# Two groups instead of three: regrouping products and blocks in a Strassen-type FFN step

## The chip, the cores and the metric

The kernel runs on one core of one Trainium2 chip. The metric is the device time of one execution in microseconds (us), of which the lower is the better. TensorE (PE in the profile; PEld is its weight loads) does the matmuls, VectorE (DVE) and ScalarE (ACT) read their results from PSUM, GpSimd (POOL) works on SBUF only, and SyncE (SP) issues the DMAs. Each engine takes its instructions in order and waits on semaphores of the others.

## The reference

A chunked attention (chunks of 64 tokens) gives 2304 tokens of 512 features. Two feed-forward layers follow; the change lies in the second, "FFN 2", a mixture of 8 experts over all tokens:

```python
logits = x @ w_gate
P = np.exp(logits - logits.max())
for _ in range(8):                      # Sinkhorn scaling: rows, then columns
    P /= P.sum(1, keepdims=True) + 1e-09
    P /= P.sum(0, keepdims=True) + 1e-09
    P *= N / E
out = np.zeros((N, D))
for e in range(E):                      # E = 8, hidden width 1024
    h = np.maximum(x @ w1[e], 0.0)
    out += P[:, e:e + 1] * (h @ w2[e])
```

All is in float32. A matmul of full precision is made of three matmuls of rounded parts: high with high, high with low, low with high.

## The kernel before

The 2304 tokens are cut into 6 blocks of 384, and FFN 2 takes them in 3 pairs of blocks. Each pair runs 32 steps (`k` counts on through the pairs), one for a quarter of an expert's hidden units: 256 of them. The first layer of a step, 256 hidden units by 2 blocks of tokens, is computed by seven matrix products of a Strassen-Winograd scheme instead of eight (`product(ps, k, i)`, i from 0 to 6, 6 matmuls each with 384 columns). The second layer of the first pair is plain: six blocks of 128 tokens by 512 features (`layer2_ffn2`, 6 matmuls of 512 columns each). The later pairs use another scheme (`step2`), which the change doesn't touch.

The function `step(k, y, hooks)` writes one step of the first pair. The order of the source is the order on each engine: the schedule is written by hand, with no planner behind it. A step computes the products of its own first layer and the six blocks of the second layer of the step before, `y(0)` to `y(5)`; so relu and splitting have most of a step's time.

- Products 0, 3 add up in PSUM tile `pa`, products 1, 4, 6 in `pb`, products 2, 5 in `pd`. In between, other engines read the tile: ACT copies `pa` after product 0 into `p1` (L739) and `pd` after product 2 into `p7` (L750), DVE adds `pb` and `p1` into `p16` after product 1 (L743) and into `p165` after product 4 (L759). The next product on the tile has to wait for that reader. The three tiles are the same three PSUM banks in each step.
- The four results of the first layer are `pa` itself after product 3, `c21` (L762), `c22` (L764) and `c12` (L774). `relu_split` makes a high part of each by ACT (L685, `gh`) and a low part by DVE (L686, `gl`).
- A block `y(n)` takes one of three PSUM buffers; DVE adds it to the output sums `acc` with the expert's weight of each token (L721, or L712 and L714 for the first two experts; in step 8 also a scaling by ACT, L705).
- `hook(0)` to `hook(9)` run small tasks handed in by the main loop. In most steps these are, for the weights of the next step: hook 0 a cast (with POOL's subtraction and a store by SP) of half of the second layer's weights and a copy of the first layer's raw weights to PSUM (L512); hook 1 one cast; hook 2 the other half and four sums by DVE (L524 to L527); hook 3 a copy to PSUM (L572) and a cast; hook 4 two casts; hook 5 four sums by DVE (L579 to L582) and a cast; hook 6 three casts; hook 7 two; hook 8 one. A cast is an ACT instruction for the high part and a POOL subtraction for the low part, both under L204 and L205, and the result goes to DRAM by an SP store, as the later pairs load it from there.
- Other hooks bring tasks of a few steps only: the Sinkhorn scaling of the gate in steps 2 to 8 (`sinkhorn_rows`, L1095 to L1099, five DVE operations, in hook 5 of steps 3, 5 and 7; `sinkhorn_cols` with a small matmul L1103), and the splitting of the second pair's x in steps 24 to 31 (`x_tasks2`, in hooks 6 and 8: sums by DVE, L650 and L652 among them, and a cast under L204).

Of the kernel before, what the change touches and what calls it, by code (L numbers as in the profile page):

```python
# [39 lines left out]
def block_attention_two_ffn_kernel(ctx, tc, shape, qk, v, w_in, w_out, w_gate, w1, w2, out, out_t):  # L40
# [74 lines left out]
    def f(ap):  # L115
        return ap.bitcast(F32)
# [368 lines left out]
    def ffn1_out(i):  # L485
        layer2_ffn1(*at(i))
        sum_ffn1(*at(i))
# [186 lines left out]
    def product(ps, k, i):  # L674
        w, (bh, bl) = wc[k, PRODUCTS[i][0]], xc[k // NU2, PRODUCTS[i][1]]
        for kk in range(2):
            for s, (a, b) in enumerate(((0, bh), (0, bl), (1, bh))):
                nc.tensor.matmul(  # L678
                    ps, w[:, a, kk, :], b[:, kk, :],
                    start=(i < 3 and kk == 0 and s == 0), stop=(kk == 1 and s == 2), skip_group_check=(i >= 3),  # L680
                )

    def relu_split(key, src):
        g2[key] = hi, lo = tuple(gp.tile([P, TB], F32R, tag=t, name=t) for t in ("gh", "gl"))
        nc.scalar.activation(hi, src, AF.Relu)  # L685
        nc.vector.scalar_tensor_tensor(lo, src, 0.0, f(hi), ALU.max, ALU.subtract)  # L686
# [3 lines left out]
    def layer2_ffn2(k, j, t, new_y=pyp.tile):  # L690

        p, u = divmod(k, NU2)
        e, b = u // UPE, 2 * p + j
        T = b * TT + t
        o = slice(t * 512, (t + 1) * 512)
        py = new_y()
        mm3(
            py,
            [(tuple(a[:, t * P:(t + 1) * P] for a in g2[k, i, j]), w2t[NU1 + k, i]) for i in range(2)],
            6,  # L700
        )
        if u == 0 and t == 0:
            acc[b] = new_acc(b)
        if p == 0 and u == 2 * UPE - 1:
            nc.scalar.activation(acc[b][:, o], acc[b][:, o], AF.Copy, scale=pm[:, T, 0:1])  # L705
        if p == 0 and u == UPE and t == 0:
            acc1[b] = new_x(1).rearrange("p k t -> p (k t)").bitcast(F32)
        a = acc[b][:, o]
        if p == 0 and e < 2:
            a = (acc, acc1)[e][b][:, o]  # L710
            if u % UPE == 0:
                nc.vector.tensor_copy(a, py)  # L712
            else:
                nc.vector.tensor_tensor(a, py, a, ALU.add)  # L714
            return
        if p == 0 and u == 2 * UPE + j * TT + t:
            nc.vector.scalar_tensor_tensor(a, acc1[b][:, o], pm[:, T, 1:2], a, ALU.mult, ALU.add)
        if u == 0:
            nc.vector.tensor_scalar(a, py, pm[:, T, 0:1], None, ALU.mult)
        else:  # L720
            nc.vector.scalar_tensor_tensor(a, py, pm[:, T, e:e + 1], a, ALU.mult, ALU.add)  # L721
        if u == NU2 - 1:
            nc.sync.dma_start(out=out[T * P:(T + 1) * P, :], in_=a)

    def step(k, y, hooks):

        t32 = lambda tag, bufs=3: tmp.tile([P, TB], F32, tag=tag, name=tag, bufs=bufs)  # L730
        tt = nc.vector.tensor_tensor
        hook = lambda n: [h() for h in hooks.get(n, ())]
        pa = new_h()
        product(pa, k, 0)
        hook(0)
        if k == 0:
            y(0)
        p1 = t32("s1")
        nc.scalar.copy(p1, pa)  # L739
        pb = new_h()  # L740
        product(pb, k, 1)
        p16 = t32("t", 2)
        tt(p16, pb, p1, ALU.add)  # L743
        hook(1)
        if k == 0:
            y(1)
        pd = new_h()
        product(pd, k, 2)
        p7 = t32("s1")
        nc.scalar.copy(p7, pd)  # L750
        hook(2)
        if k:
            y(0)
        hook(3)
        product(pa, k, 3)
        relu_split((k, 0, 0), pa)
        product(pb, k, 4)
        p165 = t32("t", 2)
        tt(p165, pb, p1, ALU.add)  # L759
        product(pd, k, 5)  # L760
        c21 = pd
        tt(c21, pd, p16, ALU.add)  # L762
        c22 = t32("z")
        tt(c22, p165, p7, ALU.add)  # L764
        relu_split((k, 1, 0), c21)
        relu_split((k, 1, 1), c22)
        hook(4)
        if k:
            y(1)
        y(2)  # L770
        hook(5)
        product(pb, k, 6)
        c12 = pb
        tt(c12, pb, p1, ALU.add)  # L774
        relu_split((k, 0, 1), c12)
        hook(6)
        y(3)
        hook(7)
        y(4)
        hook(8)  # L780
        y(5)
        hook(9)
# [465 lines left out]
    for k in range(NU2):  # L1248
        hooks = {}
        hook = lambda n, task: hooks.setdefault(n, []).append(task)  # L1250
        if k == 0:
# [3 lines left out]
            y = lambda n: ffn1_out(NS1 - LAG + n)  # L1255
        else:
            y = lambda n: layer2_ffn2(k - 1, n // TT, n % TT)
# [30 lines left out]
        for n in range(10):  # L1288
            if (k, n) in steps:
                hook(n, steps[k, n])  # L1290
        step(k, y, hooks)
    yx.close()
    y2x = ExitStack()
# [63 lines left out]
```

## Time and profile before

| what | value |
|---|---|
| runs | 1914.67, 1915.0, 1915.12 us; median 1915.0 us |
| profiled execution | 1914.93 us, span 1913.1 us |
| granted TensorE clock, mean | 0.998 |
| PE busy | 1889.2 us (99%) |
| DVE busy | 1542.4 us (81%) |
| POOL busy | 1369.0 us (72%) |
| ACT busy | 890.0 us (47%) |

The 32 steps of the first pair run from 450 us to 963 us of the span. A time of a matmul in the trace is its latency; matmuls overlap, so the cost of a group is read from the start of its first matmul to the start of the next group's first. In a time line, like instructions that follow each other stand in one row with their number, and a note in brackets tells how long the engine had been idle and who released it.

### The profile page before, as it was taken

How to read it: one execution, taken by the hardware profiler on the slowest of the kernel's cores; microseconds unless marked ns; L12 is line 12 of the kernel's file. 1: busy time of each engine (PE TensorE's matmuls, PEld its weight loads, DVE VectorE, ACT ScalarE, POOL GpSimd, SP SyncE). 2: the span in 40 equal slices, each digit the busy share in tenths (PEclk: the TensorE clock that was granted, in tenths of full speed). 3: DMA queues.
4: the chain of work that ended last, by engine and by line, in shares of the span. 5: the costliest groups of instructions: out<-in, count | busy, mean ns of one | idle time of the engine just before them, and what ended most of it. 6: DMA issues, size and time to landing. Idle time of an engine off the chain costs nothing.

```text
span 1913.1 us, 35096 instructions
## 1 busy us (share of the span) xinstructions
PE 1889.2 (99%) x11522; PEld 1821.7 (95%) x11522; DVE 1542.4 (81%) x2575; ACT 890.0 (47%) x2043; POOL 1369.0 (72%) x1400
## 2 busy tenths in 40 slices
PE   6999999999999999999999999999999999999998
PEld 5999999999899889999999999999999999999998
DVE  8998787866898887778858888888777888777777
ACT  6877777765555555555532222232223222222322
POOL 5635767665666766667767778787778877777776
PEclk9999999999999999999999999999999999999999
DMA  7411111103788888888898888888888888888883
GB/s 265 136 65 45 45 45 45 40 17 117 286 293 301 307 306 301 304 297 305 295 354 286 257 252 260 262 262 258 253 258 259 261 281 274 253 261 262 262 252 121
DMA packets 256997, 430.49 MB, mean 225 GB/s; under 512 B 26000, under 2 KB 81328, under 8 KB 256816
## 3 DMA queue, kind: packets, MB, share of 16 engines
q1 hardware_dynamic: 256816, 428.25, 68.2%
q8 instruction: 93, 1.52, 0.3%
q14 instruction: 88, 0.72, 0.1%
HBM read 304.89 MB, written 123.26 MB: 224 GB/s over the span
## 4 chain that ended last, share of the span: by engine, by line
PE 92%; DVE 5%; POOL 1%; ACT 1%; issue 1%; DMA 1%; DVEq 0%; SPq 0%; POOLq 0%; ACTq 0%
PE h L678 36%; PE y L837 23%; PE y L370 23%; PE h L370 9%; DMA raw<-in_moe_w_in 1%; DVE sm L303 0%; PE t L370 0%; DVE ex L294 0%; DVE mx L286 0%; DVE x L355 0%; DVE s L418 0%; DVE cvm L188 0%; POOL gl L205 0%; DVE s L442 0%; DVE s L413 0%
## 5 line engine op out<-in xcount | busy, mean ns | idle before, releaser
L678 PE MATMUL h<-x,wa 128*128 128x384 f32 x4032 | 789.8, 335 | 0.0
L678 PEld LDWEIGHTS h<-x,wa 128*128 128x128 f32 x4032 | 709.0, 188 | 9.7 <-issue 0.6
L837 PE MATMUL y<-gh,wb 128*128 128x384 f32 x1764 | 519.1, 334 | 1.4 <-DVE acc L842 0.6
L842 DVE TENSOR_TENSOR acc<-y,acc 128x768 f32<-128x768 f32 x367 | 348.9, 953 | 133.8 <-PE y L837 132.5
L205 POOL TENSOR_TENSOR gl<-cvm,gh 128x384 fp32r<-128x384 f32 x252 | 261.7, 1038 | 137.8 <-ACT gh L204 137.8
L837 PEld LDWEIGHTS y<-gh,wb 128*128 128x128 f32 x1764 | 324.8, 188 | 3.8 <-ACT gh L204 1.9
L837 PE MATMUL y<-gl,wb 128*128 128x384 f32 x882 | 294.7, 334 | 0.0
L204 ACT CAST gh<-cvm 128x384 fp32r<-128x384 f32 x252 | 129.3, 513 | 293.4 <-DVE cvm L873 166.0
L204 ACT CAST gh<-z 128x384 fp32r<-128x384 f32 x189 | 97.0, 513 | 347.0 <-POOL z L889 225.6
L370 PE MATMUL y<-wb,gh 128*128 128x512 f32 x768 | 238.9, 392 | 0.0
L205 POOL TENSOR_TENSOR gl<-z,gh 128x384 fp32r<-128x384 f32 x189 | 197.8, 1047 | 45.4 <-ACT gh L204 40.4
L370 PE MATMUL h<-x,wa 128*128 128x384 f32 x1152 | 216.3, 336 | 0.4 <-DVE t L428 0.3
L370 PEld LDWEIGHTS h<-x,wa 128*128 128x128 f32 x1152 | 200.2, 188 | 1.6 <-DVE t L428 0.8
L370 PE MATMUL y<-gh,wb 128*128 128x384 f32 x708 | 194.4, 336 | 0.8 <-DVE acc L481 0.8
L423 POOL TENSOR_TENSOR s<-s,s 128x384 f32<-128x384 f32 x91 | 95.4, 1049 | 103.4 <-DVE s L418 76.4
L370 PEld LDWEIGHTS y<-wb,gh 128*128 128x128 f32 x768 | 142.4, 188 | 25.6 <-issue 0.4
L837 PEld LDWEIGHTS y<-gl,wb 128*128 128x128 f32 x882 | 165.6, 188 | 0.0
L370 PE MATMUL y<-wb,gl 128*128 128x512 f32 x384 | 151.2, 394 | 0.0
L205 POOL TENSOR_TENSOR wa<-cvm,wa 128x256 fp32r<-128x256 f32 x128 | 99.6, 778 | 67.3 <-ACT wa L204 64.4
L370 PEld LDWEIGHTS y<-gh,wb 128*128 128x128 f32 x708 | 129.1, 188 | 3.0 <-issue 1.9
L685 ACT ACTIVATE gh<-h 128x384 fp32r<-128x384 f32 x96 | 47.2, 492 | 178.2 <-DVE h L774 97.5
L370 PE MATMUL y<-gl,wb 128*128 128x384 f32 x354 | 118.3, 334 | 0.0
(224 smaller groups left out, 3119.0 us busy)
## 6 DMA issues: line engine op xcount, KB each, us to landing
wa<-w1d SPq DMA_DIRECT2D x448, 256.0 KB, 3.1
wb<-w2d SPq DMA_DIRECT2D x441, 256.0 KB, 3.1
w1d<-wa SPq DMA_DIRECT2D x224, 256.0 KB, 3.2
w2d<-wb SPq DMA_DIRECT2D x192, 256.0 KB, 3.6
raw<-in_moe_w SPq DMA_DIRECT2D x33, 512.0 KB, 4.1
wb<-in_moe_w SPq DMA_DIRECT2D x62, 256.0 KB, 4.8
qk<-in_qk SPq DMA_DIRECT2D x18, 512.0 KB, 4.9
raw<-in_moe_w_in SPq DMA_DIRECT2D x16, 512.0 KB, 3.6
```

What stands on the lines that cost most here:

```text
L204: nc.scalar.copy(hi, src)
L205: nc.gpsimd.tensor_tensor(lo, src, f(hi), ALU.subtract)
L370: nc.tensor.matmul(ps, lhsT, rhs, start=(i == 0), stop=(i == n - 1))
L423: eng.tensor_tensor(s1, s1, w, ALU.mult)
L678: nc.tensor.matmul(ps, w[:, a, kk, :], b[:, kk, :], start=(i < 3 and kk == 0 and s == 0), stop=(kk == 1 and s == 2), skip_group_check=(i > ...
L685: nc.scalar.activation(hi, src, AF.Relu)
L837: nc.tensor.matmul(y[:, c, :], w[:, a, c, :], b, start=(s == 0), stop=(s == 2))
L842: nc.vector.tensor_tensor(m, y, m, ALU.add)
```

## The change

In a step of the first pair, product 3 and its relu move ahead of the first block, and blocks 1 and 2 with hook 4 move ahead of products 4 and 5. So products and blocks stand as 4, 3 blocks, 3, 3 blocks instead of 3, 1 block, 3, 2 blocks, 1, 3 blocks. Products 4, 5 and 6 with their readers, hooks 5 to 9 and blocks 3 to 5 stay behind them in the old order. Step 0, whose blocks belong to the FFN before and in which `y(0)` and `y(1)` stand further ahead, only moves product 3 ahead of hook 3, and hook 4 and `y(2)` ahead of product 4.

```diff
         p7 = t32("s1")
         nc.scalar.copy(p7, pd)
         hook(2)
+        product(pa, k, 3)
+        relu_split((k, 0, 0), pa)
         if k:
             y(0)
         hook(3)
-        product(pa, k, 3)
-        relu_split((k, 0, 0), pa)
+        if k:
+            y(1)
+        hook(4)
+        y(2)
         product(pb, k, 4)
         p165 = t32("t", 2)
         tt(p165, pb, p1, ALU.add)
...
         tt(c22, p165, p7, ALU.add)
         relu_split((k, 1, 0), c21)
         relu_split((k, 1, 1), c22)
-        hook(4)
-        if k:
-            y(1)
-        y(2)
         hook(5)
         product(pb, k, 6)
         c12 = pb
```

## Rows read from the trace of the kernel before

**Rows 1.** The page, its first part: busy us, share of the span, instructions by engine.

```profile
PE 1889.2 (99%) x11522; PEld 1821.7 (95%) x11522; DVE 1542.4 (81%) x2575; ACT 890.0 (47%) x2043; POOL 1369.0 (72%) x1400
```

**Rows 2.** Time line of PE, step 20: start, us, operation, tiles, count.

```profile
775.85 3.31 PE L678 MATMUL h<-x,wa 128*128 128x384 f32 x18
778.99 0.63 PE L370 MATMUL y<-wb,gh 128*128 128x512 f32 x2
...
780.38 3.29 PE L678 MATMUL h<-x,wa 128*128 128x384 f32 x18
783.51 0.63 PE L370 MATMUL y<-wb,gh 128*128 128x512 f32 x2
...
786.27 1.23 PE L678 MATMUL h<-x,wa 128*128 128x384 f32 x6
787.33 0.63 PE L370 MATMUL y<-wb,gh 128*128 128x512 f32 x2
...
791.45 1.05 PE L678 MATMUL h<-x,wa 128*128 128x384 f32 x5
```

**Rows 3.** Waits, 440 to 980 us: who waited for whom, total us, times, longest.

```profile
ACT gh L685 <- DVE h L774: 97.5, 32, 4.4
```

**Rows 4.** Time line of DVE, and one row of ACT, step 20.

```profile
782.66 0.56 DVE L759 TENSOR_TENSOR t<-h,s 128x384 f32<-128x384 f32 x1
783.70 0.57 DVE L762 TENSOR_TENSOR h<-h,t 128x384 f32<-128x384 f32 x1 [0.48 <-PE h L678]
...
785.79 1.43 DVE L721 SCALAR_TENSOR_TENSOR acc<-y,pm,acc 128x512 f32<-128x512 f32 x2
787.13 0.41 DVE L579 TENSOR_TENSOR cve<-wq,wb 128x256 f32<-128x256 f32 x1
...
788.59 0.56 DVE L774 TENSOR_TENSOR h<-h,s 128x384 f32<-128x384 f32 x1
...
789.18 0.49 ACT L685 ACTIVATE gh<-h 128x384 fp32r<-128x384 f32 x1 [2.98 <-DVE h L774]
```

**Rows 5.** Time line of ACT, from L774's reader in step 28 to the next copy.

```profile
914.28 0.49 ACT L685 ACTIVATE gh<-h 128x384 fp32r<-128x384 f32 x1 [2.96 <-DVE h L774]
...
916.50 0.83 ACT L204 CAST x<-acc 128x768 fp32r<-128x768 f32 x1
917.24 0.62 ACT L204 CAST wb<-wb 128x512 fp32r<-128x512 f32 x1
...
918.28 0.47 ACT L739 COPY s<-h 128x384 f32<-128x384 f32 x1
```

**Rows 6.** Time lines of DVE and of PEld, second pair: a weight load that waited.

```profile
1548.12 0.94 DVE L842 TENSOR_TENSOR acc<-y,acc 128x768 f32<-128x768 f32 x1
...
1549.13 0.19 PEld L837 LDWEIGHTS y<-gh,wb 128*128 128x128 f32 x1 [0.24 <-issue]
```

**Rows 7.** Time lines of DVE, step 7, and of PE, step 6: gate work.

```profile
584.98 0.30 DVE L1095 TENSOR_REDUCE rs<-pm 128x18 f32<-128x144 f32 x1
...
586.52 0.56 DVE L774 TENSOR_TENSOR h<-h,s 128x384 f32<-128x384 f32 x1
...
566.73 0.28 PE L1103 MATMUL sm<-cs,ident 128*128 128x8 f32 x2
```

**Rows 8.** Time line of ACT, step 8.

```profile
602.36 0.72 ACT L705 ACTIVATE acc<-acc,pm 128x512 f32<-128x512 f32 x1
602.99 0.39 ACT L204 CAST wb<-z 128x256 fp32r<-128x256 f32 x1
```

**Rows 9.** Time line of ACT, from step 25 into step 26.

```profile
867.41 0.49 ACT L685 ACTIVATE gh<-h 128x384 fp32r<-128x384 f32 x1 [2.96 <-DVE h L774]
...
870.87 0.52 ACT L204 CAST x<-s 128x384 fp32r<-128x384 f32 x1 [1.14 <-DVE s L652]
871.29 0.62 ACT L204 CAST wb<-wb 128x512 fp32r<-128x512 f32 x1
...
872.33 0.47 ACT L739 COPY s<-h 128x384 f32<-128x384 f32 x1
```

## The prediction

> **What bounds the kernel now.** I read the page first: TensorE (PE) is busy 99% of the span [rows 1]. That says little by itself, so next I read the time line of PE over one step of the first pair (step 20, a plain one). The reader should see that its rows follow each other without an idle note: 18 matmuls of products, 6 of blocks, 18 of products, 12 of blocks, 6 of products, 18 of blocks, and then the next step [rows 2]. So in this stage PE waits for nobody, and a new order of the same matmuls can gain only what the borders between groups cost. It can lose as soon as some wait reaches PE. For that I read what waits elsewhere: ScalarE (ACT) waits longest for L774, the sum that follows the last product, 97.5 us in 32 times [rows 3]. ACT takes its work in order, so everything behind that wait is late too; today PE doesn't notice. The question is whether it will.
>
> I write P0 to P6 for the seven products and y0 to y5 for the six blocks. Before: P0 P1 P2, y0, P3 P4 P5, y1 y2, P6, y3 y4 y5. After: P0 P1 P2 P3, y0 y1 y2, P4 P5 P6, y3 y4 y5. No instruction is added or removed.
>
> **Part one, the borders.** From the starts in [rows 2]: three products after a long run of blocks take 778.99 - 775.85 = 3.14; one product after such a run takes 787.33 - 786.27 = 1.06; so a further product takes (3.14 - 1.06) / 2 = 1.04. One block alone takes 780.38 - 778.99 = 1.39, two take 786.27 - 783.51 = 2.76, three 791.45 - 787.33 = 4.12, so a third takes 1.36. The three products after the single block take 3.13. Before, a step is 3.14 + 1.39 + 3.13 + 2.76 + 1.06 + 4.12 = 15.60. After, it is (3.14 + 1.04) + 4.12 + 3.14 + 4.12 = 15.56. That is 0.04 less, and over 31 steps 1.2 us. The Trainium skill's page "TensorE: Matmul & The Clock Gate" (Back-to-back issue gap) gives the spacing of isolated warm matmuls by the moving width alone, 518 cycles for 512 columns; by that rule a border costs nothing, the saving is 0, and the sum below would come out 1.2 us higher. The rows disagree, since the same block takes 1.39 at a border and 1.36 behind two others.
>
> **Part two, the wait that moves onto the path.** P3 adds onto the tile that P0 filled, so it waits for ACT's copy of that tile (L739). Before, y0 stood between P2 and P3 and gave the copy 1.39 us more. After, P3 follows P2 at once. At the same time P4 and P5 come later in the step, while P6 and y3 to y5 stay. So the DVE work behind P5 gets squeezed in front of L774, ACT starts its chain of casts later, and the copy comes later just where it is wanted sooner. The loop, from the start of P5 in one step to the earliest P3 in the next:
>
> P5 starts two products after the run that began at 780.38, at 780.38 + 2 * 1.04 = 782.46. DVE's sum L762 starts at 783.70, that is 1.24 later. From there L762, L764 and the two lower halves (L686) hold DVE until 785.79: 2.09. After the change the two sums onto acc (L721) have already been done, and the four sums of the second layer's weights (L579 to L582) follow, 788.59 - 787.13 = 1.46. Then L774, and ACT's upper half of it 789.18 - 788.59 = 0.59 later [rows 4]. From that ACT instruction to the copy L739 stand six casts of weights, one cast of the next step's plain weights and one copy. In step 28 this takes 918.28 - 914.28 = 4.00 back to back, with a cast of x in it that plain steps don't have, 917.24 - 916.50 = 0.74 [rows 5]: 3.26 for a plain step. The copy takes 0.47 [rows 5]. A weight load of PE that had idled, and that I take to have waited for the DVE sum just ended, started 1549.13 - (1548.12 + 0.94) = 0.07 behind it, and takes 0.19 itself [rows 6]: 0.26. The sum is 1.24 + 2.09 + 1.46 + 0.59 + 3.26 + 0.47 + 0.26 = 9.37.
>
> PE's own work over the same stretch is P5, P6, y3 to y5 and the next P0 to P2: 1.04 + 1.04 + 4.12 + 3.14 = 9.34. So a plain step stalls 0.03: the loop just closes, and everything that lengthens it is paid in full. I found these lengthenings:
>
> - Steps 3, 5 and 7 have the five row operations of the Sinkhorn scaling in hook 5, right ahead of L774: 586.52 - 584.98 = 1.54. PE has a small product of the gate in this stretch, at most 0.28, as cover [rows 7]. 1.54 - 0.28 + 0.03 = 1.29, three times: 3.9. P1 would take a share of it, since its tile waits for L774's readers.
> - In step 8, blocks y3 to y5 each bring a scaling of acc to ACT (L705), 602.99 - 602.36 = 0.63 each [rows 8]; they stand in the chain of casts: 1.9.
> - In steps 24, 27, 28 and 29 hook 8 casts 768 columns of the next pair's x: 0.74 each, 3.0 [rows 5].
> - In step 25 that cast is of a difference which DVE makes only then, and the chain is 872.33 - 867.41 = 4.92, that is 1.66 over the plain one. In step 26 the cast of 384 columns takes 871.29 - 870.87 = 0.42 [rows 9]. Together 2.1.
> - Some 20 plain steps at 0.03: 0.6.
>
> The stalls come to 3.9 + 1.9 + 3.0 + 2.1 + 0.6 = 11.5. Less 1.2 of borders, +10.3.
>
> What else is moved: P3's relu and its split come ahead of y0's sum onto acc, and hooks 3 and 4 ahead of P4. Hook 3 holds a copy and a cast, hook 4 two casts, and with them the POOL subtractions and the stores of the split weights on SP's queue. They are nearly 2 us after and under 1 us ahead of their old places on PE's clock, and nothing of the same step waits for them: I cost them at nothing. Their cover is a step's distance, as each split product is read one step later; without it each cast would be worth 0.3 to 0.4 of ACT. Blocks y0 to y5 keep three PSUM buffers with at least as long between uses: nothing.
>
> Two costs can't be read from the trace. The first is P6's wait for L759, DVE's sum that reads P4 before P6 adds onto the same tile. Before, two blocks stood between; after, only P5. L759 starts 782.66 - 781.42 = 1.24 after P4, its width costs 0.56 as L774's does, and 0.26 to PE: 2.06 [rows 4, 6], against 2.08 or a little more for P4 and P5. It fits by a hair if DVE is free when P4 ends. Lower bound 0; upper bound one sum onto acc in its way, (787.13 - 785.79) / 2 = 0.67 [rows 4]. I take 0, as the three blocks ahead of P4 give DVE 1.36 for every 0.67 of work. The second is steps 0 to 2, whose task lists differ (the FFN 1 tail, the gate): I take 0, bounds -0.5 (a block's border and some) and +1.5 (one Sinkhorn set [rows 7]).
>
> **The rivals.** *The copy is in time, so only the borders count.* The loop of 9.37 carries rounding and one release time taken from the second pair; were it 0.3 shorter, the plain steps would not stall, and with slack left over the longer ones would stall less. For it to win, the copy has to be done everywhere before P3's weight load: 1914.93 - 1.2 = 1913.7, not slower. It decides at a loop of 9.34. Against it: the long loops exceed that by 0.4 to 1.9, ten times a step's rounding. Chance 0.13.
>
> *P6 waits as well.* If DVE is late at L759, because the sums for y0 to y2 and the four sums of hook 2 pile up, P6 slips by some 0.3 in most steps, 28 * 0.3 = 8 on top of the forecast: 1933. For it: the margin is 0.02. Against it: DVE has idle time between the sums. Chance 0.08.
>
> *The order isn't the machine's.* If the program were reordered, nothing would change: 1915. ACT's rows stand in the order of the source, so chance 0.02.
>
> **How the numbers follow.** The profiled execution took 1914.93 for a span of 1913.1, and the median of the runs is 1915.0, so one sum serves both: 1914.93 + 10.3 = 1925.2, in round figures 1925. My own case, stalls of 4 to 17 us, has 0.77. Its low end is the long loops with 0.3 taken off each and no stall in the plain ones (about 1920); its high end adds 0.67 in a third of the steps (about 1932). The range 1917 to 1934 leaves out the first rival, the reordering, and a tail on the far side. A measurement of this kernel tells about 0.2%, 3.8 us, from no change: slower has 0.77 + 0.08, less 0.02 for stalls at the low end of my case, 0.83; same has the first rival's 0.13 and the reordering's 0.02 less a share for faster, 0.14; faster, which would need three times what all saved borders give, has 0.03.
>
> **What would show it.** If I am right, the PE time line shows 24, 18, 18 and 18 matmuls, the waits show PE's weight loads of h (L678) held by ACT's L739, with over a microsecond in step 9 (after L705), in steps 4, 6 and 8, and in step 26; plain steps last 15.6; in them the copy L739 starts near 3.14 - 0.26 - 0.47 = 2.4 us after P0, and L774 near 14.2 after P0 instead of 788.59 - 775.85 = 12.74. If plain steps last 15.57 and the long ones too, the first rival holds. If P6 shows waits for L759, the second does. A stall before y0, y1 or y2 would be something that I haven't thought of.

## The result, and the profile after

The changed kernel takes 1927.62 us (median of 6 runs, 1926.37 to 1928.8), the kernel before, measured beside it, 1914.79 us (6 runs, 1913.84 to 1915.12). The ratio is 1.0065, with a 95% interval of 1.0055 to 1.0075: slower by 12.8 us. The profiled execution of after has a span of 1926.3 us, 13.2 more than before.

The page of after first: its first part answers to [rows 1], and of its fifth part the weight loads of the products (busy us, mean ns of one | idle time ahead of them and what ended most of it). The last row is the same line of the page of before.

```profile
PE 1892.7 (98%) x11522; PEld 1821.5 (95%) x11522; DVE 1554.9 (81%) x2575; ACT 887.7 (46%) x2043; POOL 1367.8 (71%) x1400
...
L678 PEld LDWEIGHTS h<-x,wa 128*128 128x128 f32 x4032 | 708.2, 188 | 18.1 <-ACT s L739 8.9
...
L678 PEld LDWEIGHTS h<-x,wa 128*128 128x128 f32 x4032 | 709.0, 188 | 9.7 <-issue 0.6
```

All instruction counts are the same; PE's busy time is 3.5 us more and the span 13.2. So most of the loss is idle time of PE. Ahead of L678's loads alone the idle time is 18.1 us over all pairs, where it was 9.7, and ACT's copy ended 8.9 of it. DVE is busy 12.5 us longer with the same instructions; the last section tells why. The waits of PE's weight loads between 500 and 990 us say where it comes from (engine, line, waited for: us, times, longest). The numbers of the lines have moved by four: DVE's sum after product 4, L759 before, is L763 now, L762 is L766; L739 and L774 are where they were.

```profile
PEld h L678 <- ACT s L739: 8.9, 10, 1.8
PEld y L370 <- ACT s L905: 2.3, 1, 2.3
PEld h L678 <- DVE t L763: 1.5, 3, 0.6
PEld h L678 <- DVE gl L686: 1.2, 2, 0.6
```

None of these lines stands in the same view of before. The first is the wait that was forecast: product 3 for the copy of product 0. The last is P1 for the readers of P6's tile, the third P6 for the sum that reads P4. The second is one that the prediction does not have: the first block of the second pair (ACT's L905, which the view names, is not what held it; the run with the old order in step 31 tells more).

A plain step (step 20) on PE, to be read against [rows 2]:

```profile
782.33 4.35 PE L678 MATMUL h<-x,wa 128*128 128x384 f32 x24
786.52 0.63 PE L370 MATMUL y<-wb,gh 128*128 128x512 f32 x2
...
790.64 3.31 PE L678 MATMUL h<-x,wa 128*128 128x384 f32 x18
...
797.90 1.40 PE L678 MATMUL h<-x,wa 128*128 128x384 f32 x7
```

Two groups of each, no idle note, and the next step starts 797.90 - 782.33 = 15.57 later: the plain step does not stall. What ACT and DVE do in it, against [rows 4, 5]:

```profile
784.77 0.48 ACT L739 COPY s<-h 128x384 f32<-128x384 f32 x1
...
796.49 0.56 DVE L774 TENSOR_TENSOR h<-h,s 128x384 f32<-128x384 f32 x1
...
797.08 0.49 ACT L685 ACTIVATE gh<-h 128x384 fp32r<-128x384 f32 x1 [2.26 <-DVE h L774]
...
800.34 0.47 ACT L739 COPY s<-h 128x384 f32<-128x384 f32 x1
```

L774 starts 796.49 - 782.33 = 14.16 after P0, where it was 12.74; the copy 2.44 after P0; ACT's chain from L774's reader to the copy takes 800.34 - 797.08 = 3.26.

The difference step by step, each step from the start of P0's first matmul to that of the next step, from the time lines of PE in both traces:

| steps | before, us | after, us | difference |
|---|---|---|---|
| 0 to 2 | 56.84 | 56.82 | -0.01 |
| 3 | 15.83 | 16.51 | +0.67 |
| 4 | 16.04 | 17.21 | +1.17 |
| 6 | 16.04 | 17.67 | +1.63 |
| 8 | 16.03 | 17.05 | +1.02 |
| 9 | 15.61 | 17.34 | +1.73 |
| 25 | 15.61 | 16.26 | +0.65 |
| 26 | 15.61 | 17.18 | +1.57 |
| 27 | 15.61 | 15.93 | +0.33 |
| 28, 29, 30 | 15.61 each | 16.47, 16.42, 16.26 | +0.87, +0.81, +0.65 |
| 32 (first of the second pair) | 15.78 | 17.96 | +2.18 |
| 5, 7, 10 to 24, 31 | e.g. 15.61 | e.g. 15.57 | -0.48 in all |

The sum over steps 0 to 33 is +12.81, the difference of the medians 12.83. Between the two profiled executions the part ahead of step 0 differs by 0.55 and the part behind step 33 by -0.17, which makes the 13.2 of the spans. The granted clock is 1.00 in all these steps of both executions, so the clock is not the cause. (Differences are taken before rounding.)

### The profile page after: what moved, and what is told of

Same layout as the page of the kernel before. It is cut to its first block, busy times and chain, and to the rows that moved or that the text cites. A ratio compares the mean times of both kernels' runs of the same rounds, so it can differ in the third digit from the quotient of the medians.

```text
span 1926.3 us, 35097 instructions
## 1 busy us (share of the span) xinstructions
PE 1892.7 (98%) x11522; PEld 1821.5 (95%) x11522; DVE 1554.9 (81%) x2575; ACT 887.7 (46%) x2043; POOL 1367.8 (71%) x1400
## 4 chain that ended last, share of the span: by engine, by line
PE 85%; DVE 7%; ACT 3%; issue 2%; POOL 2%; DMA 1%; SPq 0%; DVEq 0%; ACTq 0%; POOLq 0%
PE h L678 32%; PE y L837 23%; PE y L370 19%; PE h L370 9%; DVE gl L686 1%; ACT wb L204 1%; ACT gh L685 0%; PE t L370 0%; DVE h L766 0%; DVE acc L714 0%; DVE ex L294 0%; DVE z L582 0%; DMA raw<-in_moe_w_in 0%; DMA w1d<-wa 0%; DVE s L418 0%
## 5 line engine op out<-in xcount | busy, mean ns | idle before, releaser
L678 PE MATMUL h<-x,wa 128*128 128x384 f32 x4032 | 788.8, 335 | 7.3 <-ACT s L739 5.6
L678 PEld LDWEIGHTS h<-x,wa 128*128 128x128 f32 x4032 | 708.2, 188 | 18.1 <-ACT s L739 8.9
L837 PE MATMUL y<-gl,wb 128*128 128x384 f32 x882 | 294.6, 334 | 0.0
L721 DVE SCALAR_TENSOR_TENSOR acc<-y,pm,acc 128x512 f32<-128x512 f32 x144 | 103.0, 744 | 23.6 <-PE y L370 22.8
```

The costliest lines, as they stand in the source:

```text
L678: nc.tensor.matmul(ps, w[:, a, kk, :], b[:, kk, :], start=(i < 3 and kk == 0 and s == 0), stop=(kk == 1 and s == 2), skip_group_check=(i > ...
L837: nc.tensor.matmul(y[:, c, :], w[:, a, c, :], b, start=(s == 0), stop=(s == 2))
```

## The experiments

Two theories of the loss stood against each other. By the first, the copy L739 is late because the chain behind L774 starts later (the blocks moved ahead) and is wanted earlier (product 3 moved ahead), so either half alone costs less than both. By the second, DVE is overloaded ahead of P4 to P6, which the blocks alone cause; P3's place then matters little. Each kernel was run on the same chip as runs of before; where a length of a step is given, it is read as in the table above.

### Product 3 alone

The kernel after, with blocks 1 and 2 and hook 4 put back behind product 5:

```diff
         hook(3)
-        if k:
-            y(1)
-        hook(4)
-        y(2)
         product(pb, k, 4)
 ...
         relu_split((k, 1, 1), c22)
+        hook(4)
+        if k:
+            y(1)
+        y(2)
         hook(5)
```

> Product 3 and its relu move ahead of the first block, blocks 1 and 2 stay behind product 5. Theory of the loop (P3 waits for ACT's copy, which is late only because the work behind P5 is squeezed in front of L774): the copy keeps its old times (1.3 us after P0 in plain steps, up to 3.5 in steps 6 to 9), so only steps 6 to 10 and 26 pay 0.2 to 0.8 us; the borders are worth nothing in this order: 1915 to 1918 us. Rival (the 1.39 us of cover that P3 loses is enough by itself): long stalls as in the changed kernel, some 1924.

It took 1915.75 us, ratio 1.0005 (0.9996 to 1.0015). Steps 6, 8, 9 and 26 are longer by 0.07, 0.19, 0.25 and 0.37, all others are as before; the sum is 0.9. PE's weight loads in the same stretch:

```profile
PEld h L678 <- ACT s L739: 1.1, 3, 0.4
```

Wanting the copy 1.39 us earlier is nearly free as long as the chain starts when it did.

### The blocks alone

After, with product 3 back behind y0:

```diff
-        product(pa, k, 3)
-        relu_split((k, 0, 0), pa)
         if k:
             y(0)
         hook(3)
+        product(pa, k, 3)
+        relu_split((k, 0, 0), pa)
         if k:
             y(1)
```

> Blocks 1 and 2 with hook 4 move ahead of product 4, product 3 stays behind the first block. Theory of the loop: the copy is as late as in the changed kernel, but P3 has 1.39 us more, so P3 stalls only in steps 9 and 26 (0.5 and 0.2); what is left are P1 in steps 4, 6, 8 (1.3 together), P6 in steps 3, 4, 6 (1.1) and the first block of step 32 (2.2): about 1920 us. Rival (the squeeze costs by itself, whatever P3 does): 1927.

It took 1925.85 us, ratio 1.006 (1.0045 to 1.0075). It is near what the second theory had, not the first: this half alone costs nearly as much as the whole, though in other places. Steps 25 and 27 to 30 are as before, so the wait for the copy is gone there, as the first theory has it. But PE's weight loads show what took its place:

```profile
PEld h L678 <- DVE t L763: 4.9, 5, 1.4
...
PEld h L678 <- ACT s L739: 0.5, 1, 0.5
```

P6 waits 4.9 us for L763, where it waited 1.5 in after. In steps 4 and 6 that wait is 1.37 and 1.35, against 0.44 and 0.45 in after: there P3 had already waited 0.61 for the copy, and while PE stood, DVE caught up. Step 4 is 1.56 longer than before, step 6 1.99: longer than in after (1.17 and 1.63). So two things are late in the long steps, DVE's sum for P6 and ACT's copy for P3, and the one that comes first in PE's order takes the wait. Step 9 is 1.73 longer, as in after, with 0.54 at P3 and 1.41 at P6. In steps 26 and 31 (0.75 and 0.91 longer) a block waits for its PSUM buffer, that is for L721, by 0.63 and 0.97; after has no such wait there. Step 32 is 2.17 longer, as in after. Each theory holds in its own steps.

### ACT's chain made shorter

After, with hook 0 (a cast and the copy L512, 1.04 us of ACT) behind L739 instead of ahead of it:

```diff
         product(pa, k, 0)
-        hook(0)
         if k == 0:
+            hook(0)
             y(0)
         p1 = t32("s1")
         nc.scalar.copy(p1, pa)
+        if k:
+            hook(0)
         pb = new_h()
```

> The changed kernel with hook 0 (one cast of 512 columns and one copy of 512, 0.53 + 0.52 us of ACT) behind the copy L739 instead of ahead of it. Theory of the loop: the copy comes 1.05 us earlier, P3's stalls shrink to some 0.9 in step 9 and 0.6 in step 26; P1, P6 and step 32 keep theirs (1.3, 1.1, 2.2), the borders give 1.0: about 1920 us. Rival (ACT's order of work isn't what makes the copy late): 1927, no change.

It took 1922.8 us, ratio 1.0044 (1.0028 to 1.0061). Steps 25 and 27 to 30 lose their stall (15.57 to 15.59), step 9 falls from +1.73 to +0.70, step 26 from +1.57 to +0.84: by 1.03 and 0.73, where ACT's chain ahead of the copy got 1.04 shorter. Steps 4 and 6 keep theirs (+1.19, +1.64), because P6 now waits there:

```profile
PEld h L678 <- DVE t L765: 2.8, 3, 1.0
...
PEld h L678 <- ACT s L739: 1.7, 2, 0.9
```

(L765 is L763, two lines further down.) This is the clearest evidence that the length of ACT's chain sets the stall in the steps with casts of x. Steps 3, 4, 6 and 32 don't hang on this chain: P6 waits 2.8 us where 1.1 was expected, which is 1.7 of the 2.8 above 1920. The rest is not in these step lengths: the profiled execution took 1920.32 us, the other three 1922.77 to 1923.56, and no trace shows where those lost it.

### The copy made longer, in both orders

A second, equal copy right behind L739, once in after and once in before; it writes the same values to the same tile.

```diff
         nc.scalar.copy(p1, pa)
+        nc.scalar.copy(p1, pa)
         pb = new_h()
```

> The changed kernel with the copy L739 made twice in each step, one behind the other: 0.38 us more of ACT ahead of product 3. Theory of the loop: in plain steps the copy ends 0.06 us ahead of P3's weight load, so they now stall 0.32 each, and the steps that stalled anyway take 0.38 more: 15 * 0.32 + 9 * 0.38 = 8.2, 1936 us. Rival (the plain steps have real slack, only the long ones are bound by the copy): 9 * 0.38 = 3.4, 1931 us.

> The kernel before with the copy L739 made twice in each step. Theory of the loop: P3 behind the first block has 1.39 us and more of slack, so 0.38 us of ACT is hidden in each step: 1915 us. Rival (ACT's time costs wherever it stands): 32 * 0.38 = 12, 1927 us.

In after: 1942.25 us, ratio 1.0143 (1.0129 to 1.0157). In before: 1914.8 us, ratio 0.9999 (0.999 to 1.0009). The same edit costs 14.6 us in the one order and nothing in the other. The time lines of ACT and PEld in a plain step of the first:

```profile
792.48 0.47 ACT L739 COPY s<-h 128x384 f32<-128x384 f32 x1
792.99 0.48 ACT L740 COPY s<-h 128x384 f32<-128x384 f32 x1
...
793.51 1.00 PEld L678 LDWEIGHTS h<-x,wa 128*128 128x128 f32 x6 [0.48 <-ACT s L740]
```

Now plain steps stall too: 16.01, that is 0.44 more than in after. The second copy comes 0.51 after the first, so 0.07 of it was spare: this is the margin of a plain step in after. The copy ends at 792.99 + 0.48 = 793.47, and the waiting load starts 0.04 later. I had expected 1936, from 0.38 between copies as between independent ones. Of the 6.25 above that, 26 waits by the missing 0.13 make 3.4; step 32 brings 1.53 and step 9 some 1.6, each behind a wait of two microseconds, with PE's clock at its lower level (last section).

### The new order in the plain steps only

```diff
+        new = 10 <= k <= 24
+        if new:
+            product(pa, k, 3)
+            relu_split((k, 0, 0), pa)
 ...
```

> The changed order in steps 10 to 24 alone, the old order in all others. Theory of the loop: none of these steps is lengthened, so only the borders count, 0.033 us each in 15 steps: 1914.3 us, with all other steps at their old lengths. Rival (the stalls are left over from one step to the next and come out later): steps 25 to 32 longer, up to 1919 us.

It took 1914.8 us, ratio 1.0 (0.9991 to 1.0008). Steps 15 to 24 are 0.03 shorter each, step 14 by 0.01, steps 11 to 13 are as before, step 10 is 0.18 longer, and the sum is -0.2. So the saved borders are there in ten of the fifteen steps, and they can't be seen in a median.

### The old order in step 31

After, with the old order where `k` is 31:

```diff
+        new = k != 31
+        if new:
+            product(pa, k, 3)
+            relu_split((k, 0, 0), pa)
 ...
+        else:
+            product(pa, k, 3)
+            relu_split((k, 0, 0), pa)
```

> The changed kernel with the old order in step 31 alone, the last step of the first pair. If the 2.2 us more in step 32 come from step 31's own squeeze (its sums onto acc come late, and the new PSUM tile of step 32 waits for them): 1925.4 us, and step 32 lasts 15.8 as before. If they are left over from the steps before: step 32 stays at 18.0, 1927.6 us.

It took 1926.2 us, ratio 1.0062 (1.0047 to 1.0077). The 1.4 us to after is within the spread of both; the step lengths decide. Step 32 is back at 15.79, and step 31 now takes 16.31, 0.71 more than before: the two orders meet there, and a block waits 0.7 us for L721. Steps 0 to 33 sum to +11.28, 1.53 less than in after. So the stall of step 32 comes from the order in step 31. How, the trace of after shows (time lines of POOL, DVE and PE, in order of time):

```profile
971.72 1.84 POOL L205 TENSOR_TENSOR x<-acc,x 128x768 fp32r<-128x768 f32 x1 [4.79 <-ACT x L204]
...
972.22 0.41 DVE L581 TENSOR_TENSOR z<-wb,wq 128x256 f32<-128x256 f32 x1
972.55 1.30 DVE L582 TENSOR_TENSOR z<-wb,cve 128x256 f32<-128x256 f32 x1
973.77 0.56 DVE L774 TENSOR_TENSOR h<-h,s 128x384 f32<-128x384 f32 x1
974.30 1.22 PE L678 MATMUL h<-x,wa 128*128 128x384 f32 x6
...
975.36 2.06 DVE L721 SCALAR_TENSOR_TENSOR acc<-y,pm,acc 128x512 f32<-128x512 f32 x3
...
977.56 0.71 PE L370 MATMUL y<-wb,gh 128*128 128x512 f32 x2 [2.04 <-DVE acc L721]
```

The blocks of the second pair use a pool of PSUM tiles (`y2`) that is opened when the first pair's pool (`yx`) closes, so the first of them waits for the last readers of the old blocks, the three sums L721. These stand behind L774. Before, they ended at 961.85 + 2.23 = 964.08, 0.95 after P0 of step 32 at 963.13. After, they end at 977.42, 3.12 after P0. Of the 2.17 between, 1.42 is the lateness of L774 that every step has, and 1.30 - 0.42 = 0.88 is L582, which met a subtraction of POOL on 768 columns of x that before was over by then; the three sums took 0.17 less. In before the same block was already on the edge (time lines of POOL, DVE and PEld of before):

```profile
957.76 1.86 POOL L205 TENSOR_TENSOR x<-acc,x 128x768 fp32r<-128x768 f32 x1 [3.48 <-ACT x L204]
...
959.93 0.42 DVE L582 TENSOR_TENSOR z<-wb,cve 128x256 f32<-128x256 f32 x1
...
961.85 2.23 DVE L721 SCALAR_TENSOR_TENSOR acc<-y,pm,acc 128x512 f32<-128x512 f32 x3
...
964.20 0.30 PEld L370 LDWEIGHTS y<-wb,gh 128*128 128x128 f32 x2 [0.17 <-issue]
```

Its load had stood idle for 0.17 us and started 0.12 after that sum's end; in after it is 977.53, 0.11 behind the sum's end. ACT's L905 started only at 964.39 in before, behind that load, so the load does not need it. With the block on the edge, any lateness of L774 in step 31 was going to be paid in full.

### One group of each

If borders gain and the loop only needs room, all seven products could stand in one group, followed by the six blocks. First in steps 10 to 31, with hooks 0 to 4 between the products and hook 5 ahead of y2:

```diff
+            product(pa, k, 3)
+            product(pb, k, 4)
 ...
+            product(pd, k, 5)
 ...
+            product(pb, k, 6)
+            tt(pb, pb, p1, ALU.add)
+            relu_split((k, 0, 1), pb)
+            y(0)
+            y(1)
+            hook(5)
+            y(2)
```

> In steps 10 to 31 all seven products stand in one group and the six blocks in another, so that L774 and ACT's chain come early in the step and the copy L739 is in time; steps 0 to 9 keep the old order. By the borders a step is 1.066 + 6 * 1.04 + 1.389 + 1.372 + 4 * 1.36 = 15.51 us instead of 15.61: 22 * 0.1 = 2.2 us less, 1912.5 us, if P6 is not held by the sum behind product 4 (some 0.05 us of margin). If P6 is held by DVE's four sums of hook 2: 0.3 to 0.6 in each of these steps, 1919 to 1926 us.

It took 1918.51 us, ratio 1.002 (1.0011 to 1.0028): missed. P6 is not held in the plain steps. They are 0.06 longer each, since block 5 waits for the PSUM buffer of block 2, whose sum L721 stands behind hook 5's four sums; steps 10 and 11, which pay 2.01 and 1.10, have longer waits of blocks for L721, up to 1.35 and 1.26 (time lines of DVE and PEld, a plain step):

```profile
792.41 0.87 DVE L582 TENSOR_TENSOR z<-wb,cve 128x256 f32<-128x256 f32 x1
793.21 2.05 DVE L721 SCALAR_TENSOR_TENSOR acc<-y,pm,acc 128x512 f32<-128x512 f32 x3
...
794.00 0.30 PEld L370 LDWEIGHTS y<-wb,gh 128*128 128x128 f32 x2 [0.28 <-DVE acc L721]
```

Then the same from step 14 on, with hook 5 behind y2:

```diff
-            hook(5)
             y(2)
+            hook(5)
             hook(6)
```

> The order of one group of products and one of blocks again, in steps 14 to 31 alone and with hook 5 (DVE's four sums of the second layer's weights) behind block 2 instead of ahead of it, so that the sum of block 2 onto acc frees its PSUM buffer before block 5 wants it. If that buffer was all that held the blocks: 15.51 us a step, 18 * 0.1 = 1.8 us less than before, 1913 us, and no wait of a block for L721 in plain steps. If DVE as a whole is too late: steps stay at 15.66, 1916 us.

On another chip it took 1914.14 us (11 runs) beside 1914.78 of before on that chip, ratio 0.9995 (0.9986 to 1.0004). Plain steps take 15.51, 0.10 less than before; steps 26 and 27 give 0.26 and 0.17 back, as do smaller waits after them; the sum over the steps is -0.54. PE's time line of a plain step:

```profile
775.47 7.47 PE L678 MATMUL h<-x,wa 128*128 128x384 f32 x42
782.77 0.63 PE L370 MATMUL y<-wb,gh 128*128 128x512 f32 x2
...
790.97 0.87 PE L678 MATMUL h<-x,wa 128*128 128x384 f32 x4
```

This is 13 us better than after, 6.2 of which after loses in steps 3 to 9, which have the old order here. Against before the interval takes in 1, so no version here is shown to beat it.

### The gate's rows moved out of the chain

After, with the rows of the Sinkhorn scaling of steps 3, 5 and 7 in hook 6, behind L774, and the columns one hook later in the next step:

```diff
+    for k in (3, 5, 7):
+        steps[k, 6] = steps.pop((k, 5))
+        cols, then = steps.pop((k + 1, 0)), steps.get((k + 1, 1))
+        steps[k + 1, 1] = lambda cols=cols, then=then: (cols(), then and then())
```

> The changed kernel with the Sinkhorn row operations of steps 3, 5 and 7 (1.54 us of DVE) in hook 6, behind L774 and its split, instead of in hook 5 ahead of it; the column part that needs them moves from hook 0 to hook 1 of the next step. Theory of the loop: L774 comes 1.5 us earlier in these steps, so the next steps 4, 6 and 8 lose their waits of P1 and P3 (1.2, 1.6 and 1.0 us over the kernel before): 3.0 to 3.8 us less than the changed kernel, 1924 us. Rival (DVE has simply too much to do in these steps, wherever the rows stand): no change, 1927.5 us.

It took 1927.76 us, ratio 1.0066 (1.0049 to 1.0083), as long as after: the expected gain did not come in the time. Step by step it came in part. Step 8 is back at 16.01. In steps 4 and 6, P1 and P3 no longer wait, but P6 does, as with the blocks alone; with step 3 it waits 4.0 us in all (time lines of DVE and PEld, step 6):

```profile
567.00 1.88 DVE L714 TENSOR_TENSOR x<-y,x 128x512 f32<-128x512 f32 x3
568.79 0.55 DVE L763 TENSOR_TENSOR t<-h,s 128x384 f32<-128x384 f32 x1
569.40 1.00 PEld L678 LDWEIGHTS h<-x,wa 128*128 128x128 f32 x6 [1.80 <-DVE t L763]
```

L763 is late because three sums of blocks stand in one row just ahead of it, behind the row operations that these steps have in hook 1. Steps 4 and 6 are 1.45 and 1.90 longer than before, instead of 1.17 and 1.63. And step 32 is 3.76 longer than before instead of 2.18, with the same wait but a lower clock behind it: the last section. Without that, the steps would sum to 0.6 less than in after, where 3.0 to 3.8 was expected.

## Why the prediction was right

The sign and the mechanism were right, and 1925 us is 2.6 short of what was measured. That the stalls forecast for steps 0 to 31 sum to what was measured is in part luck, as errors in them cancel; and one stall was missed. The stalls of a step below are its difference in the table plus the 0.03 that its borders save.

**The borders.** Worked out as 0.04 a step from [rows 2]. Measured: 0.03 in a step that has no stall, in after and in the run with the plain steps alone, but not in every such step: some 0.85 in all, not 1.2.

**The loop of a plain step.** It was summed to 9.37 against PE's 9.34, and so to a stall of 0.03. Two of its terms can be read again: ACT's chain of 3.26 came out as summed, and L774 came 14.16 after P0, where 14.2 was said. The term that was mis-sized is the 0.26 for PE's release. It was put together from a load of the second pair that started 0.07 after its releaser [rows 6], and a load's 0.19. In after, the copy ends at 800.34 + 0.47 = 800.81 and P3 starts at 797.90 + 3.14 = 801.04, 0.23 later; the run with two copies shows that 0.07 of this is spare, which leaves 0.16 for the release. So the first rival was right about the plain steps, and wrong about the rest: a loop without stall leaves almost nothing over for the long steps.

**The casts of x.** Steps 25 and 28 to 30 were to stall by 3.0 in all [rows 5]; they did by 3.1, from 0.69 to 0.90 each. Steps 26 and 27 were to stall by 2.1 [rows 9]; they did by 2.0. The weight load that waits in step 26, with the copy ahead of it (ACT, PEld):

```profile
880.56 0.47 ACT L739 COPY s<-h 128x384 f32<-128x384 f32 x1
...
881.08 0.99 PEld L678 LDWEIGHTS h<-x,wa 128*128 128x128 f32 x6 [1.63 <-ACT s L739]
```

**The scalings of acc, L705.** 1.9 from [rows 8]; 1.76 in step 9. It is P3's longest wait, and over a microsecond as said:

```profile
612.68 1.00 PEld L678 LDWEIGHTS h<-x,wa 128*128 128x128 f32 x6 [1.81 <-ACT s L739]
```

**The gate's rows, and P6.** Three rows of 1.29 were to cost 3.9 in steps 4, 6 and 8 [rows 7], and P6's wait for L759 was taken as 0, between 0 and 0.67. The loads that waited in these steps (PEld; steps 3, 4, 6 and 8 in order):

```profile
519.07 1.01 PEld L678 LDWEIGHTS h<-x,wa 128*128 128x128 f32 x6 [0.62 <-DVE t L763]
528.39 1.01 PEld L678 LDWEIGHTS h<-x,wa 128*128 128x128 f32 x6 [0.61 <-ACT s L739]
536.07 0.99 PEld L678 LDWEIGHTS h<-x,wa 128*128 128x128 f32 x6 [0.44 <-DVE t L763]
559.21 2.04 PEld L678 LDWEIGHTS h<-x,wa 128*128 128x128 f32 x12 [0.58 <-DVE gl L686]
561.85 0.99 PEld L678 LDWEIGHTS h<-x,wa 128*128 128x128 f32 x6 [0.61 <-ACT s L739]
569.53 1.01 PEld L678 LDWEIGHTS h<-x,wa 128*128 128x128 f32 x6 [0.45 <-DVE t L763]
592.68 2.06 PEld L678 LDWEIGHTS h<-x,wa 128*128 128x128 f32 x12 [0.58 <-DVE gl L686]
595.33 0.99 PEld L678 LDWEIGHTS h<-x,wa 128*128 128x128 f32 x6 [0.59 <-ACT s L739]
```

P1 and P3 wait 1.19 in step 6 and 1.17 in step 8, a tenth under 1.29, with P1 taking a share as said. In step 4 they wait 0.61 only: in step 3 P6 had waited 0.62, and PE's own lateness counts against the loop's. Together these are 2.97, not 3.9. P6 waits 0.62, 0.44 and 0.45, in all 1.51, which was costed at nothing. So the second rival, P6 waits as well, was right in three steps of 31, at most 0.62 in each and within the bound of 0.67; in plain steps DVE was free. The term of 3.9 and the 0 were both off, and their sum, 4.5 measured, is 0.6 off.

What holds DVE ahead of L763 is not in the sum. In steps 4 and 6 another set of the gate's row operations, which the list of hooks ahead of the prediction leaves out, stands in hook 1, and DVE has no idle time from there to L763. In step 3 it is above all one sum of hook 2, L527, which met a subtraction of POOL (DVE, step 3, before and after; with product 3 alone moved it stays at 0.42):

```profile
511.64 0.42 DVE L527 TENSOR_TENSOR cvm<-raw,cvm 128x256 f32<-128x256 f32 x1
...
513.69 1.50 DVE L527 TENSOR_TENSOR cvm<-raw,cvm 128x256 f32<-128x256 f32 x1
```

**Step 32** is the step of the prediction that failed: 2.18 us that it does not have. Its sum has no term for what comes behind step 31, and it takes the blocks' PSUM buffers to cost nothing; a stall ahead of a block was to be something not thought of. Here a block waits for PSUM, the first of the second pair, whose tile takes the place of the first pair's buffers. L774's lateness was known (1.4 us), and the 0.17 of idle in front of that block's load was in the trace of before; nobody who read only plain steps would see it.

In all: stalls forecast 11.5; measured 4.6 + 1.8 + 3.1 + 2.0 = 11.5 in steps 0 to 31, and 2.2 in step 32. The two 11.5 agree by luck: 0.6 of the forecast is for plain steps that did not stall and 0.9 too much for the gate's rows, and P6's 1.5 makes up for both. What is left of the 2.6 is step 32 and some 0.35 of borders that were not saved. The order is the machine's, as the waits show, so the last rival falls.

What stays open: steps 1, 2 and 11 to 13 don't show the 0.03 each that the others save, some 0.2 in all. In the run with ACT's chain shorter, steps 11 to 13 do show it, so there the copy seems to take it back; steps 1 and 2 were not followed.

## What to carry to other kernels

When an engine that is never idle gets its work regrouped, close the loop through the other engines once for a plain step and then once for every step that has one more task in the chain: a saving of 0.03 a step is lost to a single step in which a chain that just closed is a microsecond longer. Look also at the hand-over to the next stage, where buffers change their owner: a short idle note there is a margin already used up. When one wait is taken away, ask what comes next in the order of the engine that waited, since its lateness is uncovered: in three of the runs above the waits of steps 4 and 6 moved from P3 to P6.

## What the runs showed of the hardware

A sum on DVE with both inputs in SBUF was held up by POOL. L582 took 1.30 us in step 31 beside a subtraction of POOL that ended at 971.72 + 1.84 = 973.56; L582 ended at 973.85, 0.29 later. Alone it takes 0.42. L581, which started 972.22 beside the same subtraction, took 0.41; one of its inputs, `wq`, lies in PSUM. L527, of two SBUF inputs as well, shows the same in plain steps: 1.27 instead of 0.42 in step 20, 12.1 us over all steps, which is nearly all of the 12.5 by which DVE is busier in after. There it costs nothing, as DVE has idle time behind it (0.22, 0.61 and 0.31 us in step 20). The Trainium skill's page "SBUF — State Buffer" (SBUF: two separate sides) says that DVE with two SBUF inputs and GpSimd share a port pair that one of them holds for a whole instruction; the trace agrees.

The same idle time of PE left its clock alone in some executions and not in others. In step 32 PE waits 2.04 us in after, and the granted clock stays 1.00; in the run with the gate's rows moved it waits as long at the same place, and then the windows show (stretch, length, busy time and count of PE, PEld, DVE, ACT, POOL, then PE's granted clock, DMA share, GB/s):

```profile
976.25:978.80 2.55, 2.55 (x6) 2.07 (x7) 0.00 (x0) 0.00 (x0) 2.22 (x2) 0.51 0.99 304
978.80:980.30 1.50, 1.50 (x7) 1.43 (x6) 0.75 (x1) 0.00 (x0) 0.00 (x0) 0.69 0.90 296
980.30:983.00 2.70, 2.70 (x15) 2.41 (x14) 1.31 (x2) 0.00 (x0) 0.00 (x0) 1.00 0.99 338
```

Right behind the wait the clock is at its lower level (0.51, 1.2 GHz), and by 980.30 it is back at 1.00. That is the 3.76 - 2.18 = 1.58 by which step 32 is longer in that run. In the run with two copies step 32 is 1.53 longer than in after, and the matmuls behind the same wait are as slow there (1.04 us for a row of two, instead of 0.71). Its step 9 shows it too: PE waits 1.99 us for the second copy, until 614.27, and then:

```profile
615.01:618.42 3.41, 3.41 (x11) 2.83 (x10) 3.38 (x6) 2.33 (x6) 2.62 (x4) 0.50 1.01 352
```

So a stall of two microseconds can cost 3.7, and a single profile doesn't tell which it will be.
